# Residual of the second attention layer's first twelve row blocks by an accumulating DMA, with another tile order in the second convolution

## The chip, the cores and the metric

The kernel runs on one core of one Trainium2 chip. The metric is the device time of one execution in microseconds; the time of the kernel before is the median of three runs.

## The reference

The kernel computes four layers on one sequence `x` of 2048 rows by 512 columns in bf16: attention, convolution, attention, convolution. Each layer adds its output to `x`.

```
x = x + _A_ref(_layernorm(x), wqkv, wo)
x = x + _B_ref(_layernorm(x), A, B, C, log_dt, Dskip)
x = x + _A_ref(_layernorm(x), wqkv, wo)
x = x + _B_ref(_layernorm(x), A, B, C, log_dt, Dskip)
```

`_A_ref` is attention with 32 heads of 16 columns over a window of 8 keys that lie 2 rows apart, softmax over those 8, and a projection `wo`. `_B_ref` is a state-space convolution over all 2048 rows: a kernel is made from `A`, `B`, `C` and `log_dt` for every column, and the sequence is convolved with it by a Fourier transform of length 4096. `u * Dskip` is added to its output.

## The kernel before, in words

**Layout.** The residual `x` stays in SBUF as `x_sb`, 128 partitions by 16 row blocks of 512 columns. A "row" below is one of these 16 blocks: 128 partitions x 512 elements, 128 KB in bf16. Row `a` holds the sequence positions 16p + a.

**Order of the work.** Four engines (DVE, ACT, PE, SP) are scheduled by hand: each engine executes its instructions in the order in which the program emits them, and waits on semaphores where an operand is not ready. An instruction that waits holds up everything behind it on its engine.

**Second attention (`LayerA.core`, layer `l == 1`).** After projections and logits comes a loop over n = 0 to 15 (L503 to L538), one row per turn, in the row order `rows = [0, 2, 1, 3, 4, ..., 15]`. A turn emits, in this order:

- DVE: `pv_mult(n)`, the products `pav` of the probabilities with the values (L404). In turns 1, 3, 5 and 7 it is followed by one more product for the last block of logits (L295). Softmax pieces of the last two blocks lie in turns 0 to 11.
- `u_begin` in turns 7, 11 and 15 (L514): mean and variance of four finished rows (0 to 3, 4 to 7, 8 to 11) from the sums `s1` and the sums of squares `s2` that ACT has made; three small DVE instructions (L133, L135, and L140 in turn 7). In turn 7 the power -1/2 is taken on GpSimd (L141), in turns 11 and 15 on ACT as Ln and Exp (L118, L119). `u_end` (L148) follows on DVE, and `u_apply` (L158 on ACT, L160 on DVE) writes the normalised rows.
- PE: `pv_sum(n)`, 32 matmuls with the identity that sum `pav` into `po` (L412); ACT copies it to `oT` (L415).
- `out_proj` of the row of the turn before (L418): PE adds the residual by one matmul of the identity with the 512 columns of `x_sb` (L422), then the four matmuls with `wo` (L424) into the PSUM tile `pq`. For rows 0 to 11, ACT copies `pq` over the row of `x_sb` and sums it (L430), then reads the row back for the sum of squares (L108). For rows 12 to 15 ACT only copies (L428), and DVE makes the statistics (L101).

After the loop a short sequence makes the statistics of rows 12 to 15 and their normalised rows; the convolution waits for the last of them.

**Tiles.** `pav`, `po`, `pq` and `oT` have two buffers each.

**Second convolution (`FftB.run`).** It follows a list of tokens, `ORDER1`, of four kinds of tiles. `U` (16 of them; L756 on PE) is the first transform, copied to SBUF by DVE (`UD`) or ACT (`UA`), L745. `u` (16; L763) is the second transform, which ACT always copies to `ub` (L818); `ub` has three buffers. `m` (16) are two DVE products of `ub` with a part of the filter spectrum (L805); a tile of `ub` is free when its `m` is done. `y` (16; L831 and L832) is the inverse transform, copied by DVE or ACT (L745). `z` (8; L856 and L857) is the last step, which adds into `x_sb` and is followed by a store of the output. Tiles U, u, y and z share four PSUM tiles in turn, so that a tile can begin when the fourth tile before it has been copied. There are two groups of eight: the first eight `y` need `m` 0 to 7, the last eight need all sixteen. In the last `z` tile, marked `B`, DVE and ACT each copy one half.

Of the kernel before, what the change touches and what calls it, by code (L numbers as in the profile page):

```python
# [20 lines left out]
P = 128  # L21
S = 2048
D = 512
# [3 lines left out]
NA = 16  # L27
NDT = 4
# [10 lines left out]
DQG = 64  # L39
# [20 lines left out]
T3 E31D x1 E30A P20 P22  # L60
"""
ORDER1 = """
UD UA UD UA UD UA UD UA UD UA UD u UD m u m UA UA u UD u u m u m u
m m UA u m u m m u u m u yA u m m u yD m yA u yA m u m yA
yA m yD yD yD yA yD yA yA yA yD yA z03D z00D z12D z02D z11D z10D z01A z13B
"""

def build_a_consts(tc, nc, cpool, tpool):
# [38 lines left out]
def row_sumsq(nc, lnst, x_row, a):  # L107
    nc.scalar.activation(lnst["junk"][:], x_row, ACT.Square, accum_out=lnst["s2"][:, a:a + 1])  # L108
# [14 lines left out]
def ln_begin(nc, pool, lnst, a0, a1, eng, rs="pool"):  # L123
    n = a1 - a0
    if eng == "dve":
        ag = pool.tile([P, n, 2], F32, name="ln_ag")
        for a in range(n):
            nc.vector.bn_aggr(ag[:, a, :], lnst["bn"][:, a0 + a, 0, :])
        var, mean, ms = ag[:, :, 1], ag[:, :, 0], -1.0
    else:  # L130
        mean, ms = lnst["s1"][:, a0:a1], -1.0 / D
        msq = pool.tile([P, n], F32, name="ln_msq")
        nc.vector.scalar_tensor_tensor(msq[:], mean, -1.0 / (D * D), mean, ALU.mult, ALU.mult)  # L133
        veps = pool.tile([P, n], F32, name="ln_veps")
        nc.vector.scalar_tensor_tensor(veps[:], lnst["s2"][:, a0:a1], 1.0 / D, msq[:], ALU.mult, ALU.add)  # L135
        var = veps[:]
    if rs == "act":
        return rstd_act(nc, pool, var), mean, ms
    rstd = pool.tile([P, n], F32, name="ln_rstd")
    nc.vector.tensor_scalar(rstd[:], var, EPS, None, ALU.add)  # L140
    nc.gpsimd.tensor_tensor(rstd[:], rstd[:], lnst["mh"][:, 0:n], ALU.pow)  # L141
    return rstd, mean, ms
# [20 lines left out]
class LayerA:  # L163
# [143 lines left out]
    def core(self, x_sb, u, lnp, ev=None, nprod=0):  # L307

        tc, nc, lnst, l = self.tc, self.nc, self.lnst, self.layer
        ident, nident = self.c["ident"], self.c["nident"]  # L310
# [11 lines left out]
        with ExitStack() as c2:  # L322
# [7 lines left out]
            wk = c2.enter_context(tc.tile_pool(name=f"a{l}_wk", bufs=2, reuse_waits="tile"))  # L330
# [87 lines left out]
            def out_proj(a):  # L418
                oT = oTs.pop(a)
                pw = pq_tile()  # L420
                xr = x_sb[:, a, :]
                nc.tensor.matmul(pw[:], lhsT=ident[:], rhs=xr, start=True, stop=False)  # L422
                for ftp in range(NDT):
                    nc.tensor.matmul(pw[:], lhsT=oT[:, ftp, :], rhs=self.wo[:, ftp, :], start=False, stop=(ftp == NDT - 1))  # L424
                if a >= 12:
                    if a >= 14 and l == 1:
                        row_stats(nc, lnst, pw[:], a, "dve")
                    nc.scalar.copy(xr, pw[:])  # L428
                else:
                    nc.scalar.activation(xr, pw[:], ACT.Identity, accum_out=lnst["s1"][:, a:a + 1])  # L430
                    row_sumsq(nc, lnst, xr, a)
# [4 lines left out]
            def u_begin(a0, a1, eng, rs="pool"):  # L436
                lns[a0] = ln_begin(nc, lnp, lnst, a0, a1, eng, rs)
# [64 lines left out]
            rows = [0, 2, 1, *range(3, NA)]  # L502
            for n in range(16):  # L503
                pv_mult(rows[n])
                if n in (0, 8):
                    mx(2 + n // 8)
                if n in (2, 10):
                    recip(2 + n // 8)
                if n in (4, 11):
                    norm_p(2 + n // 8)  # L510
                if n in (1, 3, 5, 7):
                    mult(3, n // 2)
                if n in (7, 11, 15):
                    u_begin(n - 7, n - 3, "act", "act" if n > 7 else "pool")  # L514
                if n in (8, 12):
                    u_end(n - 8)
                if n in (9, 10, 13, 14):
                    b0 = 0 if n < 11 else 4
                    r0 = b0 + (0 if n in (9, 13) else 2)
                    u_apply(b0, range(r0, r0 + 2))  # L520
                if n == 15:
                    x_stats(12)
                event(("p", n))
                if n in (1, 3, 5):
                    q_proj(3, n // 2 + 1)
                pv_sum(rows[n])
                if n in (0, 8):
                    sub_exp(2 + n // 8)
                if n == 15:
                    x_stats(13)  # L530
                    if l == 1:
                        u_end(8)
                        u_apply(8, range(8, 12), "dve")
                if n > 0:
                    out_proj(rows[n - 1])
                if n in (1, 3, 5, 7):
                    lsum(3, n // 2)
                event(("o", n))  # L538
# [7 lines left out]
            pw = pq_tile()  # L546
# [159 lines left out]
class FftB:  # L706
# [129 lines left out]
    def i2(self, g, t, eng):  # L836

        nc, x_sb = self.nc, self.x_sb
        z = self.S[g]["z"]
        dsl = slice(g * DQG * 4, (g + 1) * DQG * 4)  # L840
        if eng == "both":
            for h, e in enumerate(("dve", "act")):
                self.i2_rows(z, t * 4 + 2 * h, 2, dsl, e)
        else:
            self.i2_rows(z, t * 4, 4, dsl, eng)

    def i2_rows(self, z, a0, n, dsl, eng):

        nc, x_sb = self.nc, self.x_sb
        p4 = self.ptile([P, n, DQG * 4])  # L850
        n_add = n if eng == "dve" else 0
        for j in range(n):
            a = a0 + j
            if j >= n_add:
                nc.tensor.matmul(p4[:, j, :], lhsT=self.ident[:], rhs=x_sb[:, a, dsl], start=True, stop=False)
            nc.tensor.matmul(p4[:, j, :], lhsT=self.g2[:, 0, a, :], rhs=z[:, a, :], start=(j < n_add), stop=False)  # L856
            nc.tensor.matmul(p4[:, j, :], lhsT=self.g2[:, 1, a, :], rhs=z[:, NA + a, :], start=False, stop=True)  # L857
        if n_add:
            xr = x_sb[:, a0:a0 + n, dsl]
            nc.vector.tensor_tensor(xr, p4[:], xr, ALU.add)  # L860
        else:
            nc.scalar.copy(x_sb[:, a0:a0 + n, dsl], p4[:])

    def run(self, order, u, done=lambda g, t: None, k=None, late=(), more={}):
        late, cnt = list(late), self.cnt
# [419 lines left out]
def kernel(  # L1285
# [16 lines left out]
    nc = tc.nc  # L1302
# [18 lines left out]
    u = xnT[:].rearrange("p t (b r) -> p (t b) r", r=64).rearrange("p q (a r) -> p q a r", r=4)  # L1321
# [4 lines left out]
    xpool = ctx.enter_context(tc.tile_pool(name="xres", bufs=1))  # L1326
# [59 lines left out]
    with tc.manual_schedule(engines=MAN):  # L1386
        la.front_open()
        ln, agg, pts = {}, {}, {}

        def front_pools():  # L1390
            fb.swap_psum()
            la.front_psum()

        def aggr(b):
            agg[b] = lnp.tile([P, 4, 2], F32, name="ln_ag")
# [22 lines left out]
        fb.run(ORDERF, None, more=front)  # L1418
        la.front_close()
# [60 lines left out]
```

## Time and profile before

| | |
|---|---|
| median of three runs | 429.74 us (429.44 to 429.82) |
| the profiled execution | 429.82 us |
| its span, first to last instruction | 428.0 us |
| so outside the span | 1.82 us |
| mean granted TensorE clock | 0.987 |
| turns of the loop in the second attention | 316.6 to 372 us of the span |
| second convolution, first matmul to end | 376.57 to 428.0 us |

How to read the profile: each engine has its own row. PE is the matrix engine (PEld its loads of weights), DVE the vector engine, ACT the scalar engine, POOL GpSimd, and SP the engine that issues the transfers (SPq its queue). Busy time is the time in which an engine executes an instruction. A row in the timeline gives the start, the duration, the engine, the line of the program, the operation, and the tiles that it writes and reads; a bracket at its end gives the idle time of the engine ahead of it and what ended it. The chain of waits is followed back from the last instruction, at each step to what released it.

### The profile page before, as it was taken

The page shows a single profiled execution, that of the slowest core. Times are in us where ns is not written, and L with a number is a line of the kernel's source. Part 1 is how long each engine was busy: PE and PEld are TensorE (multiplying, and loading weights), DVE is VectorE, ACT ScalarE, POOL GpSimd, SP SyncE. Part 2 cuts the span into 40 slices and gives each one's busy share as a digit, 9 for nine tenths or more (in the row PEclk, how much of TensorE's full clock was granted, in tenths as well). Part 3 has the DMA queues.
Part 4 walks back from the last instruction along what each step waited for, and adds up shares of the span by engine and source line. Part 5 has one row for each costly group of instructions (what it writes and reads, how often), then busy time and mean ns, then how long its engine had stood idle before and what let it go on. Part 6 is the DMA issues. An engine that isn't in the chain of part 4 may idle for free.

```text
span 428.0 us, 12737 instructions
## 1 busy us (share of the span) xinstructions
PE 353.1 (82%) x5506; PEld 264.9 (62%) x5506; DVE 398.1 (93%) x540; ACT 320.9 (75%) x551; POOL 43.9 (10%) x46
## 2 busy tenths in 40 slices
PE   3000159999999899999998999999999999996994
PEld 2000127667755577767887888555666777776993
DVE  8999999999999999996999959899999999899974
ACT  6999998986454389887999978855556568689941
POOL 3000300000598000001300000000000020000000
PEclk9999998999999999999999999999999999998998
DMA  8930732132116743662245592820041056416306
GB/s 213 385 114 12 81 78 69 33 62 64 24 42 186 237 113 107 215 257 102 77 175 188 190 335 43 255 82 2 20 110 46 2 217 240 131 58 175 124 4 196
DMA packets 62466, 54.16 MB, mean 127 GB/s; under 512 B 33893, under 2 KB 50890, under 8 KB 61130
## 3 DMA queue, kind: packets, MB, share of 16 engines
q1 hardware_dynamic: 62266, 53.22, 40.9%
q8 instruction: 43, 0.70, 0.7%
q10 hardware_dynamic: 144, 0.13, 0.2%
q14 instruction: 13, 0.11, 0.1%
HBM read 30.28 MB, written 13.24 MB: 102 GB/s over the span
## 4 chain that ended last, share of the span: by engine, by line
PE 42%; DVE 25%; ACT 10%; issue 4%; DMA 3%; SPq 2%; DVEq 0%; ACTq 0%
PE po L412 7%; DVE pav L404 7%; PE pk L1174 4%; DVE prod L295 4%; DVE a1s L745 4%; PE pq L351 4%; PE pq L424 4%; PE pp L1112 3%; PE pp L242 3%; PE L L302 3%; PE pq L185 3%; DVE t L805 3%; ACT ub L818 2%; PE pb L832 2%; PE pb L831 2%
## 5 line engine op out<-in xcount | busy, mean ns | idle before, releaser
L404 DVE TENSOR_TENSOR pav<-attn,v_ext 128x4096 bf16<-128x4096 bf16 x32 | 72.9, 2282 | 0.0
L295 DVE TENSOR_TENSOR prod<-qT,kT_ext 128x4096 bf16<-128x4096 bf16 x29 | 66.4, 2307 | 0.2
L412 PEld LDWEIGHTS <-pav 128*128 128x128 bf16 x1024 | 58.4, 98 | 12.2 <-DVE pav L404 8.6
L412 PE MATMUL po<-ident,pav 128*128 128x128 bf16 x1024 | 62.5, 219 | 3.8 <-DVE pav L404 3.3
L1102 PE MATMUL pt<-ident,x_blk 128*128 128x128 bf16 x64 | 6.9, 258 | 43.4 <-ACT x_blk L158 43.4
L1014 DVE TENSOR_TENSOR A_t<-A_t,pow_t 128x1024 bf16<-128x1024 bf16 (+4 forms) x46 | 38.4, 873 | 0.2
L1102 PEld LDWEIGHTS <-x_blk 128*128 128x128 bf16 x64 | 5.3, 116 | 46.1 <-ACT x_blk L158 44.4
L818 ACT CAST ub<-pb 128x1024 bf16<-128x1024 f32 x32 | 32.9, 1079 | 1.1 <-PE pb L763 0.5
L763 PE MATMUL pb<-a1s,w_sb 128*128 128x64 bf16 x768 | 29.1, 197 | 5.1 <-ACT a1s L745 2.7
L353 ACT CAST v_ext<-pq 128x512 bf16<-128x512 f32 x32 | 18.8, 586 | 19.3 <-PE pq L351 18.0
L424 PE MATMUL pq<-wop,oT 128*128 128x512 bf16 x128 | 32.8, 379 | 0.0
L302 PEld LDWEIGHTS <-prod 128*128 128x128 bf16 x928 | 27.1, 96 | 8.8 <-DVE prod L295 3.2
L832 PE MATMUL pb<-WpJ,t 128*128 128x128 bf16 x256 | 29.8, 219 | 1.9 <-DVE t L805 1.9
L415 ACT CAST oT<-po 128x512 bf16<-128x512 f32 x32 | 18.6, 580 | 17.0 <-PE po L412 16.9
L745 DVE CAST a1s<-pb 128x1024 bf16<-128x1024 f32 x23 | 27.0, 1214 | 4.3 <-PE pb L756 4.3
L763 PEld LDWEIGHTS <-w_sb 128*128 128x128 bf16 x768 | 26.3, 101 | 7.5 <-issue 5.8
L1112 PE MATMUL pp<-xnT,kT_ext 128*128 128x512 bf16 x96 | 26.6, 405 | 5.2 <-ACT qT L1117 3.2
L831 PE MATMUL pb<-Wp,t 128*128 128x128 bf16 x256 | 30.1, 219 | 0.8 <-ACT ub L818 0.4
L351 PE MATMUL pq<-wv,xnT 128*128 128x512 bf16 x128 | 30.7, 379 | 0.0
L302 PE MATMUL L<-ind,prod 128*128 128x8 bf16 x928 | 27.4, 166 | 1.3 <-DVE prod L295 1.2
L832 PEld LDWEIGHTS <-t 128*128 128x128 bf16 x256 | 24.9, 98 | 3.2 <-DVE t L805 2.1
L745 ACT CAST a1s<-pb 128x1024 bf16<-128x1024 f32 x25 | 24.7, 1033 | 2.3 <-PE pb L756 2.0
(227 smaller groups left out, 863.1 us busy)
## 6 DMA issues: line engine op xcount, KB each, us to landing
w_sb<-w_dram SPq DMA_DIRECT2D x8, 1024.0 KB, 7.6
w_dram<-w_zero SPq DMA_DIRECT2D x1, 4096.0 KB, 14.6
kf_ring<-kf_dram SPq DMA_DIRECT2D x13, 256.0 KB, 3.8
kf_ring<-kf_dram SPq DMA_DIRECT2D x26, 128.0 KB, 3.6
v_ext<-v_ext SPq DMA_DIRECT2D x4, 784.0 KB, 6.2
x_blk<-in_A_x_dram SPq DMA_DIRECT2D x4, 512.0 KB, 4.3
kT_ext<-in_A_wqkv_dram SPq DMA_DIRECT2D x4, 512.0 KB, 10.0
x_sb<-in_A_x_dram SPq DMA_DIRECT2D x4, 512.0 KB, 5.3
```

What stands on the lines that cost most here:

```text
L295: nc.vector.tensor_tensor(pr, self.qT[q][:, ft].unsqueeze(1).to_broadcast([P, W, 4, P]), kap, ALU.mult)
L302: self.nc.tensor.matmul(L[:, al, w, ft * 8:(ft + 1) * 8], lhsT=pr[:, w, al, :], rhs=self.c["ind8"][:], start=(ft == 0 and w == 0 and al % ...
L351: nc.tensor.matmul(pp[:], lhsT=xnT[:, dt, a * P:(a + 1) * P], rhs=wv[:, dt, :], start=(dt == 0), stop=(dt == NDT - 1))
L404: nc.vector.tensor_tensor(pv[:], attn[:, n % 4].unsqueeze(2).to_broadcast([P, W, DH, H]), vap, ALU.mult)
L412: nc.tensor.matmul(po[:, ft, :], lhsT=pvf[:, w, ft * P:(ft + 1) * P], rhs=ident[:], start=(w == 0 and ft == 0), stop=(w == W - 1), skip_gr ...
L424: nc.tensor.matmul(pw[:], lhsT=oT[:, ftp, :], rhs=self.wo[:, ftp, :], start=False, stop=(ftp == NDT - 1))
L745: (self.nc.scalar.copy if eng == "act" else self.nc.vector.tensor_copy)(dst, src)
L763: nc.tensor.matmul(p2[:, j, :], lhsT=self.w2[:, ec * EC + j, :], rhs=a1s[:, ec * EC + j, :], start=True, stop=True)
L818: nc.scalar.copy(ub[:], p2)
L831: nc.tensor.matmul(p3[:, j, :], lhsT=t1[:, dql, :], rhs=wp_r, start=True, stop=False)
L832: nc.tensor.matmul(p3[:, j, :], lhsT=t2[:, dql, :], rhs=wpj_r, start=False, stop=True)
L1112: nc.tensor.matmul(pps[kind, b, ft][:], lhsT=la.wqk[:, dt, c:c + P], rhs=la.xnT[:, dt, b * 512:(b + 1) * 512], start=(dt == 0), stop=(dt = ...
```

## The change

For rows 0 to 11 of the second attention layer the identity matmul (L422) is left out. ACT copies `pq`, now without the residual, to a new tile `ow` with two buffers, and sums it on the way; GpSimd issues a DMA that adds `ow` to the row of `x_sb`. The sum of squares of a row is no longer made directly behind the copy, but two turns later, from the row of `x_sb` that the DMA has written. Since `s1` now holds only the sum of the added part, the mean of the row as it was is kept from the front of the layer (`mean0`) and added by one more DVE instruction in each `u_begin`. In turn 7 the power is taken on ACT instead of GpSimd. In the convolution the token list is another one, and the tile marked `B` is one PSUM tile of four rows instead of two of two rows.

```
 ORDER1:
-UD UA UD UA UD UA UD UA UD UA UD u UD m u m UA UA u UD u u m u m u
-m m UA u m u m m u u m u yA u m m u yD m yA u yA m u m yA
-yA m yD yD yD yA yD yA yA yA yD yA z03D z00D z12D z02D z11D z10D z01A z13B
+UD UA UA UD UA UA UD UA UD UA UD u UD u m UA u u m UA m u u UA m UD m
+u u m m m u u m u m m u u m u m m u yA yA yA m u yA yA yA yA
+m yD yA yD yD yA z00D yD yA z01D yA yA z02D z03D z10D z11D z12A z13B
 ln_begin:
         mean, ms = lnst["s1"][:, a0:a1], -1.0 / D
+        if "mean0" in lnst:
+            nc.vector.scalar_tensor_tensor(mean, lnst["mean0"][:, a0:a1, 0], float(D), mean, ALU.mult, ALU.add)
 out_proj:
-                nc.tensor.matmul(pw[:], lhsT=ident[:], rhs=xr, start=True, stop=False)
+                by_dma = l == 1 and a < 12
+                if not by_dma:
+                    nc.tensor.matmul(pw[:], lhsT=ident[:], rhs=xr, start=True, stop=False)
...
+                if by_dma:
+                    ow = wk.tile([P, D], BF16, name="ow")
+                    nc.scalar.activation(ow[:], pw[:], ACT.Identity, accum_out=lnst["s1"][:, a:a + 1])
+                    nc.gpsimd.dma_start(xr, ow[:], accum_op=ALU.add)
+                elif a >= 12:
 the loop over n:
-                    u_begin(n - 7, n - 3, "act", "act" if n > 7 else "pool")
+                    u_begin(n - 7, n - 3, "act", "act" if n > 7 or l else "pool")
...
                 if n > 0:
                     out_proj(rows[n - 1])
+                if l == 1 and 3 <= n < 15:
+                    row_sumsq(nc, lnst, x_sb[:, rows[n - 3], :], rows[n - 3])
 i2:
+        p4 = self.ptile([P, 4, DQG * 4])
+        n_add = {"dve": 4, "both": 2, "act": 0}[eng]
...
+        if n_add:
+            xr = x_sb[:, t * 4:t * 4 + n_add, dsl]
+            nc.vector.tensor_tensor(xr, p4[:, 0:n_add], xr, ALU.add)
+        if n_add < 4:
+            nc.scalar.copy(x_sb[:, t * 4 + n_add:t * 4 + 4, dsl], p4[:, n_add:4])
```

More of the change, by code (lines that the diff above doesn't have):

```diff
@@ L421, in out_proj @@
                 xr = x_sb[:, a, :]
-                nc.tensor.matmul(pw[:], lhsT=ident[:], rhs=xr, start=True, stop=False)
+                by_dma = l == 1 and a < 12
+                if not by_dma:
+                    nc.tensor.matmul(pw[:], lhsT=ident[:], rhs=xr, start=True, stop=False)
                 for ftp in range(NDT):
-                    nc.tensor.matmul(pw[:], lhsT=oT[:, ftp, :], rhs=self.wo[:, ftp, :], start=False, stop=(ftp == NDT - 1))
-                if a >= 12:
+                    nc.tensor.matmul(pw[:], lhsT=oT[:, ftp, :], rhs=self.wo[:, ftp, :],
+                                     start=(by_dma and ftp == 0), stop=(ftp == NDT - 1))
+                if by_dma:
[3 more added lines that the diff above has]
+                elif a >= 12:
                     if a >= 14 and l == 1:
@@ L840, in i2 @@
         dsl = slice(g * DQG * 4, (g + 1) * DQG * 4)
[L841 to L853, printed above, removed]
+        p4 = self.ptile([P, 4, DQG * 4])
+        n_add = {"dve": 4, "both": 2, "act": 0}[eng]
+        for j in range(4):
+            a = t * 4 + j
             if j >= n_add:
@@ L858, in i2_rows @@
         if n_add:
[L859 to L862, printed above, removed]
+            xr = x_sb[:, t * 4:t * 4 + n_add, dsl]
+            nc.vector.tensor_tensor(xr, p4[:, 0:n_add], xr, ALU.add)
+        if n_add < 4:
+            nc.scalar.copy(x_sb[:, t * 4 + n_add:t * 4 + 4, dsl], p4[:, n_add:4])
     def run(self, order, u, done=lambda g, t: None, k=None, late=(), more={}):
@@ L1388 @@
         ln, agg, pts = {}, {}, {}
+        mean0 = xpool.tile([P, NA, 2], F32, name="ln_mean0")
         def front_pools():
@@ L1394, in aggr @@
         def aggr(b):
-            agg[b] = lnp.tile([P, 4, 2], F32, name="ln_ag")
+            agg[b] = mean0[:, 4 * b:4 * b + 4, :]
             for a in range(4):
@@ L1418 @@
         fb.run(ORDERF, None, more=front)
+        lnst["mean0"] = mean0
         la.front_close()
```

## Prediction

> **What bounds the kernel now.** I read the table of stretches first, then the chain of waits around the changed loop, then the timelines of single engines. In the stretches the columns are: stretch, its length, busy time of PE, PEld, DVE, ACT and POOL, TensorE clock, DMA share and GB/s.
>
> ```profile
> 348.00:355.00 7.00, 6.88 (x96) 5.13 (x93) 6.94 (x7) 5.21 (x12) 1.46 (x1) 1.00 0.99 415
> 355.00:361.00 6.00, 5.87 (x75) 4.38 (x73) 5.92 (x8) 5.30 (x15) 0.00 (x0) 1.00 0.45 184
> 361.00:367.00 6.00, 5.96 (x76) 4.57 (x75) 6.00 (x7) 4.58 (x11) 0.00 (x0) 1.00 0.79 243
> 367.00:376.50 9.50, 9.17 (x90) 5.92 (x88) 7.64 (x21) 5.86 (x14) 0.00 (x0) 1.00 0.36 124
> ```
>
> In the loop DVE is without a gap until its last product ends at 368.55, and PE is nearly as full. So work taken from PE pays only where PE, and not DVE, comes last. The chain (start, length, what) says where:
>
> ```profile
> 355.97 2.19 DVE pav L404
> ...
> 358.21 1.96 PE po L412 x32
> 360.17 0.22 PE pq L422
> 360.39 0.88 PE pq L424 x4
> ...
> 361.28 1.96 PE po L412 x32
> ...
> 372.96 0.71 DVE ln_bn L101
> ```
>
> `po` of turn 11 (358.21) starts when DVE's product is ready, and so does that of turn 12 (361.28: the product of 358.94 ends at 361.22). Whatever PE saves earlier is lost in these waits. From 361.28 on PE sets the pace to 372.96, where DVE's statistics of row 14 begin exactly as PE finishes; the convolution starts at 376.57, 3.6 us behind them.
>
> **The identity matmuls.** One of 512 columns takes 0.22 us of the chain. Twelve go: 12 x 0.22 = 2.6 us of PE. Eleven lie ahead of 361.28, under DVE, and give nothing. Only row 11's, in turn 12, lies behind it: -0.22 us. The waits of PE on DVE grow by the rest.
>
> **The late sums of squares.** The sum of squares of row 7 was done in turn 8; now ACT makes it in turn 10, behind the copy of row 9, and `u_begin` of turn 11 needs it. These are DVE's and ACT's rows there:
>
> ```profile
> 358.07 0.68 DVE L394 TENSOR_TENSOR attn<-ex,rs 128x1024 bf16<-128x1024 bf16 x1
> 358.67 0.15 DVE L133 SCALAR_TENSOR_TENSOR ln_msq<-ln_s 128x4 f32<-128x4 f32 x1
> 358.86 0.16 DVE L135 SCALAR_TENSOR_TENSOR ln_veps<-ln_s,ln_msq 128x4 f32<-128x4 f32 x1
> 358.94 2.28 DVE L404 TENSOR_TENSOR pav<-attn,v_ext 128x4096 bf16<-128x4096 bf16 x1
> ```
> ```profile
> 358.31 0.60 ACT L430 ACTIVATE x_sb<-pq 128x512 bf16<-128x512 f32 x1
> 358.80 0.20 ACT L430 ACTIVATION_READ_ACCUMULATOR x_sb<-pq 128x1 f32 x1
> 359.03 0.63 ACT L108 ACTIVATE ln_junk<-x_sb 128x512 bf16<-128x512 bf16 x1
> 359.57 0.19 ACT L108 ACTIVATION_READ_ACCUMULATOR ln_junk<-x_sb 128x1 f32 x1
> ```
>
> ACT has no idle time from 350.64 but 0.48 us at 355.25, where it waits for PE; an identity matmul less ends this 0.2 us sooner. So its slot for a sum of squares in turn 10 ends at 359.76 - 0.2 = 359.55. DVE, which is in order, waits there with L135 and starts the product of turn 12 at 359.75 instead of 358.94: +0.8 us (this holds the added L133-like instruction of 0.15 us, which runs in the wait). That product is on the chain, so turn 13 starts 0.8 - 0.22 = 0.57 us late, and PE carries this to turn 15.
>
> In turn 15 the same happens with row 11. Its sum of squares now stands behind ACT's copy of row 13, which was at 370.09 and comes at 370.66. It starts at 371.15 and ends some 0.7 us later (0.63 and 0.19, overlapping), at 371.86; DVE's L135 then ends at 372.05, where it was over at 368.8. Behind it wait two statistics (0.6 us each of DVE's time: 373.25), L148 (0.1) and four rows of L160 (1.39): 374.8. Only then can the statistics of row 14 begin, at 372.96 before: +1.85 us, the 0.57 included. What follows is the same chain of 3.6 us. In turn 7, L135 waits until about 345.95, where it ran at 346.03: nothing, with 0.1 us either way.
>
> **The power in turn 7.** ACT gets 0.4 us (Ln and Exp, 0.2 each) ahead of `oT` of turn 7. Behind that copy ACT has 1.49 us idle ahead of 350.64: hidden. Without this cover it would cost 0.4.
>
> **The DMA.** Twelve transfers of 128 KB, SBUF to SBUF, from a queue that the trace of before does not show. They must land in time for ACT: the copy of row a+2 overwrites the tile `ow` of row a, and the sum of squares of row a follows that copy. From the end of one copy to the start of the copy two turns later are 5.0 to 7 us (352.75 to 358.1 for row 7). The nearest rows:
>
> ```profile
> kn<-kn SPq DMA_DIRECT2D x8, 128.0 KB, 2.1
> ...
> kx<-kf_dram SPq DMA_DIRECT2D x4, 128.0 KB, 3.9
> ```
> ```profile
> 170.90 1.02 POOL L141 TENSOR_TENSOR ln_rstd<-ln_rstd,ln_mh 128x4 f32<-128x4 f32 x1 [33.16 <-DVE ln_rstd L140]
> ...
> 346.57 2.89 POOL L141 TENSOR_TENSOR ln_rstd<-ln_rstd,ln_mh 128x4 f32<-128x4 f32 x1 [98.19 <-DVE ln_rstd L140]
> ```
>
> From below: 2.1 us (the same size inside SBUF, idle queues), no cost. From above: twice the busy row, 7.8 us, since the destination is read as well, and 1.9 us because GpSimd's own instruction took 2.89 instead of 1.02 us where a `pav` product ran beside it: 9.7 us. Then a copy comes only every (9.7 + 0.8) / 2 = 5.25 us, against 3.45 us in turns 2 to 12 ((363.08 - 328.57) / 10): 10 x 1.8 = +18 us. I take about 4.5 us, near the busy row plus half a microsecond for GpSimd, and so no cost. Of the two loads beside it, the one of 346 to 356 (0.99 of all DMA engines) makes this least sure. Past POOL's queue nothing is moved; the L141 that stood there is gone.
>
> [...]
>
> **The convolution.** DVE gets one U tile and two y tiles less (1.14 us each), ACT that much more (0.96 each). The end of the last `m` decides when the second eight `y` can start. Before:
>
> ```profile
> 401.90 4.89 DVE L805 TENSOR_TENSOR t<-ub,kf_ring 128x1024 bf16<-128x1024 bf16 x8
> ```
> ```profile
> 403.68 1.09 ACT L818 CAST ub<-pb 128x1024 bf16<-128x1024 f32 x1
> 404.58 2.02 ACT L745 CAST xnT<-pb 128x1024 bf16<-128x1024 f32 x2
> ```
>
> ACT's last `ub` is done at 404.8, DVE's last `m` at 406.8, PE goes on at 406.85. I followed the new list with the durations above, four PSUM tiles and three `ub`. The first `m` starts as before (385.1), DVE then runs 16 `m` of 1.22 and one U, and the `ub` of `m` n waits for `m` n-3: `u` 14 is copied by 402.0. But now three `yA` stand on ACT between it and `u` 15 (402.0 to 404.9), which is done at 405.8: the last `m` ends at 407.0, although DVE has less to do. Four more `yA` follow on ACT until 409.6, and the ninth `y` needs the PSUM tile of the second of them, so PE starts it at 407.8: +0.95 us. From there PE has 8 `y` and 8 `z` of 0.86 us in either list, and the end moves by the same. The two ends: -2.3 us if DVE's lighter load (1.14 x 2 ahead of the last `m`) reached the end, +2 us if all seven `yA` of group 0 delay it. The joined `B` tile changes nothing that I can price above 0.2 us.
>
> **The sum.** Against the profiled execution of 429.82 us (0.08 above the median): 1.85 + 0.95 = 2.8, so 432.6 us.
>
> **Rivals.**
> 1. The transfers land late, and `ow`'s two buffers make ACT wait in turns 3 to 12. It decides from 5.0 us of landing, turn by turn, and in all turns from 6.1 us ((6.1 + 0.8) / 2 = 3.45). At 7 us, between 5.8 (3.9 + 1.9) and 7.8 (twice 3.9), it gives 10 x ((7 + 0.8) / 2 - 3.45) = +4.5 on top, 437.1; at 8 us +9.5, 442. For it: DVE without a gap, full DMA engines. Against: 2.1 to 3.9 us for all such sizes in the trace.
> 2. GpSimd holds DVE up. Beside POOL's L696 the product L295 took up to 2695 ns instead of 2283, and L381 828 instead of 417: 0.41 us for each of 12 issues would be +4.9, 437.5. [...]
> 3. Not slower: the convolution gives its 2.3 us, because ACT's three `yA` are through ahead of `u` 15. It decides if `u` 14 is copied by 400.5 instead of 402.0. With the attention's 1.85 the end is 429.4; if the wait of turn 15 is hidden too, 428.1.
> 4. The change doesn't do what it says: PE is not shorter in the turns, because it waits for DVE as much longer. That holds for eleven of the twelve rows in my forecast already; for the twelfth it is 0.22 us, 432.8, inside the forecast's own range and its chance.
>
> **How the numbers follow.** Forecast (430.7 to 434.5): 0.52. Rival 1: 0.24. Rival 2: 0.08. Rival 3: 0.16, half of it faster. A difference of 0.2%, 0.86 us, is about what a measurement of this kernel can tell from no change, so faster means below 428.9 and slower above 430.6: 0.08, 0.08, 0.84. The range takes rival 3's 429.4 and half of rival 1: 429.2 to 439.5. The forecast's own range is 430.7 to 434.5.
>
> **What would show it.** Right: DVE idle of about 0.8 us ahead of L135 in turn 11 and of 2 to 3 us in turn 15, ended by ACT's sum of squares; PE waits for `pav` that grow to 0.2 us more a turn; landing times under 5 us; `u` 15 copied behind three `y`. Wrong: ACT idle ahead of the copy to `ow`, ended by a DMA; `pav` above 2.3 us; an end of the convolution stage within 51 us of its start.

## The result, and the profile after

The changed kernel takes 435.65 us (median of four, 435.4 to 437.45), beside 429.78 us (429.44 to 430.36) for the kernel before on the same chip: a ratio of 1.0144, interval 1.0115 to 1.0174. (Here and below the ratio is the recorded one, with its 95% interval; it is not exactly the quotient of the two medians.) It is slower by 5.9 us; the forecast was 2.8 us slower, 432.6 us. The sign was right and the size too small by half. The profiled execution took 435.77 us, its span 434.0 us, so 1.8 us lie outside as before.

I cut the two spans at the same events: the start of the product `pav` of turn 0 of the loop, `po` of turns 12 and 15, the first matmul of the convolution, and the last instruction. (Lines of the changed kernel have other numbers: `pav` is L406, `po` L414, the copy to `ow` L432, its DMA L433; inside `u_begin` the instruction that waits for the sums of squares was L135 and is now L137.)

| us | before | after | difference |
|---|---|---|---|
| start of the span to turn 0 | 316.60 | 314.94 | -1.66 |
| turn 0 to `po` of turn 12 | 44.68 | 48.91 | +4.23 |
| `po` of turn 12 to `po` of turn 15 | 8.61 | 11.22 | +2.61 |
| `po` of turn 15 to the convolution | 6.68 | 7.80 | +1.12 |
| convolution, first matmul to end | 51.43 | 51.13 | -0.30 |
| span | 428.0 | 434.0 | +6.0 |

So the loop alone lost 8.0 us. The first thing to look at is the landing of the twelve accumulating transfers. This is the group's line in the list of DMA issues of the changed kernel (last number: median us from issue to landing):

```profile
x_sb<-ow POOLq DMA_DIRECT2D x12, 128.0 KB, 4.5
```

The median is the 4.5 us that I forecast, and it misleads. One by one, in the order of the rows 0, 2, 1, 3, 4, ... 11, they took 4.4, 2.7, 2.7, 2.7, 2.6, 5.1, 7.6, 8.6, 5.1, 4.6, 5.2 and 3.3 us. The two slow ones, rows 6 and 7, were issued at 346.58 and 351.39 us, beside a load of 4 MB that is issued at 344.4 us for the convolution. The chain of waits (start, length, what) goes straight through row 7's:

```profile
351.39 8.63 DMA x_sb<-ow
...
360.10 0.69 ACT ow L432 x2
360.79 0.62 ACT ln_junk L108 x2
361.41 0.02 issue
361.43 0.16 DVE ln_veps L137
361.60 2.21 DVE pav L406
363.80 0.05 issue
363.85 3.60 PE po L414 x32
```

Row 7's transfer lands at 360.02. Only then may ACT write row 9 into the same one of the two `ow` buffers; behind that copy, in order, stands row 7's own sum of squares; for it waits DVE's L137 in turn 11; and behind L137 stands the product of turn 12, for which PE waits. The waits show both ends of it, with the total, the number and the longest in us:

```profile
DVE ln_veps L137 <- ACT ln_junk L108: 6.8, 2, 4.2
...
ACT ow L432 <- DMA x_sb<-ow: 4.1, 2, 2.8
```

The table of stretches of the changed kernel (stretch, length, busy PE, PEld, DVE, ACT, POOL, granted TensorE clock, DMA share, GB/s) shows what comes with the stall and after it:

```profile
345.00:356.00 11.00, 9.98 (x145) 7.57 (x143) 10.93 (x11) 7.58 (x21) 2.26 (x3) 1.00 1.03 355
356.00:364.00 8.00, 2.97 (x38) 2.25 (x39) 3.80 (x8) 4.63 (x14) 1.52 (x3) 0.93 0.68 177
364.00:370.00 6.00, 6.00 (x48) 4.90 (x47) 4.92 (x4) 1.40 (x4) 0.52 (x1) 0.52 0.70 207
```

Before, DVE was busy for 5.92 of the 6 us from 355 to 361 and PE for 5.87. Now DVE is busy for 3.80 of 8 us. The third row is a second loss: PE is busy all the time, but its clock is granted at 0.52 only, behind the pause that it made. PE's own rows give the pause in the bracket and the matmuls at half speed, 3.60 us where `po` takes 1.96:

```profile
356.45 1.96 PE L414 MATMUL po<-ident,pav 128*128 128x128 bf16 x32 [0.56 <-DVE pav L406]
358.25 1.03 PE L428 MATMUL pq<-wop,oT 128*128 128x512 bf16 x4
363.85 3.60 PE L414 MATMUL po<-ident,pav 128*128 128x128 bf16 x32 [4.58 <-DVE pav L406]
367.24 1.91 PE L428 MATMUL pq<-wop,oT 128*128 128x512 bf16 x4
```

Turn 15 is as forecast. L137 waits for row 11's late sum of squares, and the four L162 and the statistics queue behind it (DVE, changed kernel):

```profile
376.51 0.16 DVE L137 SCALAR_TENSOR_TENSOR ln_veps<-ln_s,ln_msq 128x4 f32<-128x4 f32 x1 [2.62 <-ACT ln_junk L108]
376.59 1.28 DVE L101 BATCH_NORM_STATS2 ln_bn<-x_sb 128x6 f32<-128x512 bf16 x2
377.79 0.14 DVE L150 SCALAR_TENSOR_TENSOR ln_nb<-ln_s,ln_rstd 128x4 f32<-128x4 f32 x1
377.97 1.38 DVE L162 TENSOR_SCALAR xnT<-x_sb,ln_rstd,ln_nb 128x512 bf16<-128x512 bf16 x4
```

In the convolution three `yA` copies do stand on ACT ahead of the last `ub`, and DVE waits for it with the last `m` (first ACT, then DVE):

```profile
407.92 2.85 ACT L756 CAST xnT<-pb 128x1024 bf16<-128x1024 f32 x3
410.63 1.06 ACT L829 CAST ub<-pb 128x1024 bf16<-128x1024 f32 x1
```
```profile
411.72 1.29 DVE L816 TENSOR_TENSOR t<-ub,kf_ring 128x1024 bf16<-128x1024 bf16 x2 [1.21 <-ACT ub L829]
```

The last copy of the stage ends 47.04 us after its start, against 45.93: +1.1. Of this 0.5 us are PE's: its tenth `y` starts 31.62 us after the stage's start, against 31.12, and its last matmul 45.43 against 44.91. The other 0.6 us are the joined `B` tile, in which ACT's half now waits for DVE's half, where before the two ended side by side at 422.4 and 422.5 us:

```profile
429.33 0.58 ACT L864 CAST x_sb<-pb 128x512 bf16<-128x512 f32 x1 [0.81 <-DVE x_sb L862]
```

Yet the stage is not longer. The nine stores of the output begin earlier against the last copy, and what follows the last copy is 4.09 us in place of 5.50. I had followed the list to the last copy and not to the last store.

### The profile page after: what moved, and what is told of

Its sections match the earlier page's. It is cut to its first block, busy times and chain, and to the rows that moved or that the text cites. A ratio compares the mean times of both kernels' runs of the same rounds, so it can differ in the third digit from the quotient of the medians.

```text
span 434.0 us, 12771 instructions
## 1 busy us (share of the span) xinstructions
PE 351.8 (81%) x5494; PEld 264.0 (61%) x5494; DVE 394.7 (91%) x539; ACT 322.0 (74%) x556; POOL 51.6 (12%) x57
## 4 chain that ended last, share of the span: by engine, by line
PE 40%; DVE 22%; issue 7%; ACT 6%; DMA 6%; SPq 2%; POOL 1%; DVEq 0%; ACTq 0%; POOLq 0%
PE pk L1176 5%; PE po L414 5%; DVE t L816 5%; DVE pav L406 5%; PE pq L353 4%; PE pp L1114 4%; DVE a1s L756 4%; DVE prod L297 3%; PE pp L244 3%; PE L L304 3%; PE pq L187 2%; PE pq L428 2%; PE pb L842 2%; PE pb L843 2%; DMA x_sb<-ow 2%
## 5 line engine op out<-in xcount | busy, mean ns | idle before, releaser
L406 DVE TENSOR_TENSOR pav<-attn,v_ext 128x4096 bf16<-128x4096 bf16 x32 | 72.9, 2282 | 2.3 <-PE po L414 2.3
L414 PE MATMUL po<-ident,pav 128*128 128x128 bf16 x1024 | 64.6, 223 | 10.2 <-DVE pav L406 10.0
L414 PEld LDWEIGHTS <-pav 128*128 128x128 bf16 x1024 | 60.4, 100 | 19.0 <-DVE pav L406 15.5
L428 PE MATMUL pq<-wop,oT 128*128 128x512 bf16 x128 | 33.7, 387 | 0.0
L774 PE MATMUL pb<-a1s,w_sb 128*128 128x64 bf16 x768 | 27.7, 193 | 4.8 <-ACT ub L829 3.5
L756 DVE CAST a1s<-pb 128x1024 bf16<-128x1024 f32 x22 | 26.1, 1216 | 5.1 <-PE pb L767 5.0
L774 PEld LDWEIGHTS <-w_sb 128*128 128x128 bf16 x768 | 24.8, 98 | 7.5 <-issue 5.9
L756 ACT CAST a1s<-pb 128x1024 bf16<-128x1024 f32 x26 | 25.6, 1043 | 2.3 <-PE pb L767 2.2
```

What stands on the lines that cost most here:

```text
L406: nc.vector.tensor_tensor(pv[:], attn[:, n % 4].unsqueeze(2).to_broadcast([P, W, DH, H]), vap, ALU.mult)
L414: nc.tensor.matmul(po[:, ft, :], lhsT=pvf[:, w, ft * P:(ft + 1) * P], rhs=ident[:], start=(w == 0 and ft == 0), stop=(w == W - 1), skip_gr ...
L756: (self.nc.scalar.copy if eng == "act" else self.nc.vector.tensor_copy)(dst, src)
L774: nc.tensor.matmul(p2[:, j, :], lhsT=self.w2[:, ec * EC + j, :], rhs=a1s[:, ec * EC + j, :], start=True, stop=True)
```

## Theories

**Theory A.** Of the loss, 4.2 us are two transfers that land late because the 4 MB load has the DMA engines; 2.6 us are TensorE's clock behind the pause; 1.1 us are row 11's late sum of squares. **Rivals:** it is the two buffers and not the data; it is GpSimd's queue and not the load; it is the accumulation; the clock falls because of the transfers and not of the pause.

In the results below, "loop" is the time from the product of turn 0 to the convolution's first matmul in the profiled execution (59.97 before, 67.93 after), with its three parts in brackets (44.68, 8.61, 6.68 before): up to `po` of turn 12, from there to `po` of turn 15, and the rest.

## Experiments: each part of the change by itself

**The token list alone,** in the kernel before:

```
-ORDER1, i2 of the kernel before
+ORDER1, i2 of the changed kernel
```

> The kernel before with only the new token list and the joined last tile. Theory A (from the trace after: the last z copy comes 1.2 us later behind the convolution's start, but the stores are spread and the end follows it 1.5 us sooner): -0.3 us, 429.5. Theory B (the forecast's price): +0.95, 430.7.

Measured: 428.83 us beside 429.04, ratio 1.0006 (0.9978 to 1.0034). The last copy comes 47.04 us after the stage's start, as in the changed kernel, and the stage takes 51.41 us (51.43 before). The list is worth nothing either way; that +0.95 did not come is read from the stage, since the interval alone would leave room for it.

**The late sums of squares alone,** in the kernel before, with no DMA:

```
-                    row_sumsq(nc, lnst, xr, a)
+                    if l == 0:
+                        row_sumsq(nc, lnst, xr, a)
...
+                if l == 1 and 3 <= n < 15:
+                    row_sumsq(nc, lnst, x_sb[:, rows[n - 3], :], rows[n - 3])
```

> The kernel before, where only the sum of squares of a row stands two turns later on ACT; no DMA, identity matmuls kept. The forecast's step: +0.8 to 1.0 us in turn 11 (DVE waits at L135) and about +1.05 in turn 15, in all +1.85 to 2.1, 431.6 to 431.9. If the moved statistics are hidden by themselves: 429.8.

Measured: 430.32 us, ratio 1.0022 (1.0003 to 1.0041); loop 61.66, +1.69 (45.25, 8.61, 7.80), so +0.57 in turn 11 and +1.12 in turn 15. DVE's two waits in this kernel:

```profile
359.05 0.16 DVE L135 SCALAR_TENSOR_TENSOR ln_veps<-ln_s,ln_msq 128x4 f32<-128x4 f32 x1 [0.67 <-ACT ln_junk L108]
...
371.51 0.16 DVE L135 SCALAR_TENSOR_TENSOR ln_veps<-ln_s,ln_msq 128x4 f32<-128x4 f32 x1 [2.70 <-ACT ln_junk L108]
```

The forecast had +1.85 with one wait of 0.8 and one of 2 to 3 us.

**No identity matmul,** in the kernel before (the residual of rows 0 to 11 is left out of the output):

```
-                nc.tensor.matmul(pw[:], lhsT=ident[:], rhs=xr, start=True, stop=False)
+                bare = l == 1 and a < 12
+                if not bare:
+                    nc.tensor.matmul(pw[:], lhsT=ident[:], rhs=xr, start=True, stop=False)
...
```

> The kernel before without the twelve identity matmuls; the residual of rows 0 to 11 is left out. The forecast's step: -0.22 us, 429.6, since DVE's products set the pace up to turn 12. If PE sets the pace in all turns: 12 x 0.22 = -2.6 us, 427.2.

Measured: 428.18 us, ratio 0.9967 (0.9949 to 0.9985); loop 59.55, -0.42 of the 2.6 us that the twelve matmuls take. In the loop this is all that leaving them out brings in this schedule, were the DMA free.

## Experiments: the load, or something else?

**DMA for rows 0 to 5 only,** which land ahead of the load or beside its first part; rows 6 to 11 as before the change (and the kept mean is added for rows 0 to 5 alone):

```
...
-                by_dma = l == 1 and a < 12
+                by_dma = l == 1 and a < 6
...
-                if l == 1 and 3 <= n < 15:
+                if l == 1 and 3 <= n and rows[n - 3] < 6:
```

> The changed kernel with the DMA for rows 0 to 5 only; rows 6 to 11 keep the identity matmul and their sum of squares directly behind the copy. Theory A: rows 0 to 5 land in 2.7 to 5 us ahead of their need, DVE waits at no statistic, and the loop is as long as before (59.6 to 60.2 us from turn 0 to the convolution), the time within 0.3% of the kernel before: half of the matmuls gone and nothing gained. Rival (the DMA itself costs, by GpSimd's 0.86 us of issue or by its traffic): at least 2 us above the kernel before.

Measured: 428.87 us beside 428.93, ratio 1.0000 (0.9984 to 1.0015); loop 60.04. The six land in 4.9, 2.7, 2.7, 2.7, 2.6 and 5.8 us, under a DVE without a gap. Half of the change costs nothing and gives nothing.

**The load later,** in turn 13, held back by a store of `s1` of row 11:

```
-        ev = {("p", 8): [lambda: la.load_w2(w2_dram)]}
+        gate = dram.tile([P, 1], F32, name="gate_dram")
+        ev = {("p", 13): [lambda: nc.sync.dma_start(gate[:], lnst["s1"][:, 11:12]), lambda: la.load_w2(w2_dram)]}
```

> The changed kernel with the load of the second-transform weights (4 MB, 0.99 of all DMA engines for 10 us) held back behind the copy of row 11 by a small store ahead of it in its queue. Theory A (the transfers land late because they share the DMA engines with that load): the transfers of rows 5 to 8, which took 5.1 to 8.6 us, land in 2.7 us as those of rows 1 to 4; no copy waits for a DMA; DVE's wait in turn 11 falls from 4.16 to about 0.8 us; PE keeps its clock (it took 3.60 us for a po of 1.96 behind a pause of 4.6 us); 5.5 to 6 us less, 429.7 to 430.5. [...]

Measured: 443.14 us, ratio 1.0301 (1.0268 to 1.0334). The landings are theory A's: rows 0 to 10 take 2.6 to 3.3 us, rows 6 and 7 2.7 us each, and `po` of turn 12 comes 45.27 us after turn 0, with a clock of 1.00. But row 11's transfer, issued at 364.48 between the store and the load, took 14.8 us, and ACT waited for it in turn 14:

```profile
379.61 0.63 ACT L108 ACTIVATE ln_junk<-x_sb 128x512 bf16<-128x512 bf16 x1 [10.03 <-DMA x_sb<-ow]
```

The load moved the stall to the row that it now meets. The experiment has a flaw: my store of 128 pieces of 4 bytes is slow itself (8.4 us to landing in the next run), so that what delays row 11 is load and store together.

**The load last,** in turn 15, behind the same kind of store (now of `s2`):

```
+        ev = {("p", 15): [lambda: nc.sync.dma_start(gate[:], lnst["s2"][:, 11:12]), lambda: la.load_w2(w2_dram)]}
```

> The changed kernel with the load of the second-transform weights held back until the sum of squares of row 11 is written, so that none of the twelve transfers meets it. Theory A (all of the loss beyond the late squares is the meeting with the load; held behind row 11's copy only, it made row 11 land in 14.8 us and cost 10 us in turn 15): all twelve land in 2.6 to 3.5 us, no copy and no sum of squares waits for a DMA, from turn 0 to the convolution 61.1 to 61.7 us (59.97 before, and 1.1 to 1.7 for the late squares), time 1 to 2 us above the kernel before. Rival: the load then comes too late for the first second-transform tile, and the convolution starts to wait: 3 us or more above.

Measured: 437.27 us, ratio 1.0197 (1.0179 to 1.0214). All rows but the first land in 2.6 to 2.9 us and the loop is 61.15, as theory A has it. But the convolution is 58.25 us, 6.8 longer, as the rival has it: the load took 18.6 us (median of its four parts) from issue to landing.

**The same with a store of one element:**

```
-        gate = dram.tile([P, 1], F32, name="gate_dram")
+        gate = dram.tile([1, 1], F32, name="gate_dram")
...
-nc.sync.dma_start(gate[:], lnst["s2"][:, 11:12])
+nc.sync.dma_start(gate[:], lnst["s2"][0:1, 11:12])
```

> The changed kernel with the 4 MB load in turn 15, held back as in the run that loads last, but by a store of one element instead of one of 128 x 1. Theory A (the transfers are late only beside the load): all land in 2.5 to 3.0 us (the first up to 5), the loop is 61.0 to 61.5 us as in the run that loads last (61.15), that is +1.2 for row 11's late sum of squares; the gate lands in about 2 us instead of 8.4, the load in 8 to 10 us instead of 18.6, so that the convolution is 51 to 53 us instead of 58.25, and the time 429.5 to 432 us. Rival (the load itself is too late in turn 15, whatever holds it back): the convolution stays above 55 us and the time above 434 us.

Measured: 430.38 us beside 428.6, ratio 1.0033 (1.0011 to 1.0054); loop 61.43 (45.23, 8.40, 7.80), convolution 51.45. The load lands in 9.8 us (median of its four parts). The list of DMA issues, the longest waits of L137, and the stretch of the stall in this kernel:

```profile
x_sb<-ow POOLq DMA_DIRECT2D x12, 128.0 KB, 2.7
```
```profile
DVE ln_veps L137 <- ACT ln_junk L108: 2.5, 2, 2.3
```
```profile
356.00:364.00 8.00, 6.67 (x91) 5.20 (x91) 7.72 (x9) 5.81 (x18) 2.58 (x3) 1.00 0.24 36
```

DVE is busy for 7.72 us where it was 3.80, and the clock stays at 1.00. With the load out of the way the changed kernel loses 1.8 us, and its loop 1.46 us: the late sums of squares (1.69 by themselves) less what the missing matmuls give (0.42) would be 1.27. So the load is the cause of the late landing, and the landing the cause of the pause and the clock. (The loads of the filter spectrum stand behind the 4 MB load in SP's queue and move with it, from 359.89 to 385.65 us. In the changed kernel row 6 had landed at 354.2 and row 7 at 360.02 us, so for these two it is the 4 MB load.)

**A plain copy in place of the accumulating one,** on the same queue (the residual is left out of rows 0 to 11):

```
-                    nc.gpsimd.dma_start(xr, ow[:], accum_op=ALU.add)
+                    nc.gpsimd.dma_start(xr, ow[:])
```

> The changed kernel with a plain copy in place of the accumulating one on the same queue; the residual of rows 0 to 11 is left out. It measures what accumulation adds. Theory A (landing is set by the shared DMA engines): alone about 2.1 to 2.7 us, beside the load as late as before, 7 to 9 us, so the time stays near 435. Rival (reading the destination is what makes it late): 4 us beside the load, and the time falls to 431 to 432.

Measured, in one execution: 431.97 us, loop 64.11 (47.91, 8.39, 7.81). The landings are 2.0 us where the accumulating ones took 2.7, and 6.7 and 7.7 for rows 6 and 7 (7.6 and 8.6). So the accumulation itself costs 0.7 to 0.9 us, and a plain copy is late too. The time is the one that I had put to the rival, though the landings are theory A's. The 0.9 us were worth more than themselves here: PE's pause was 3.61 us in place of 4.58, and behind it the clock stayed at 1.00.

**The plain copy from SP's queue:**

```
-                    nc.gpsimd.dma_start(xr, ow[:], accum_op=ALU.add)
+                    nc.sync.dma_start(xr, ow[:])
```

> The same plain copy, issued from SP's queue, where the load is issued too; the residual of rows 0 to 11 is left out. Theory A (shared engines): row 6 lands late also from this queue, 5 us or more, and row 7, which stands behind the load in the same queue, not before the load is through, near 355 us of the span. [...]

Measured, in one execution: 436.36 us, loop 68.77. ACT's copy waits even longer:

```profile
361.22 0.60 ACT L432 ACTIVATE ow<-pq 128x512 bf16<-128x512 f32 x1 [4.85 <-DMA x_sb<-ow]
```

Row 6 was issued just ahead of the load and landed in 2.0 us; there my expectation missed. Rows 7 and 8, issued behind it on the same queue, are the late ones. From another queue the transfers beside the load are late as well; but since they also stand behind the load in that queue, this run alone does not acquit GpSimd's. The run with the store of one element does: from GpSimd's queue, under the same products of DVE, all rows but the first land in 2.6 to 2.8 us once the load is gone.

## Experiments: which wait, and can it be mended?

**Four buffers of `ow`:**

```
-                    ow = wk.tile([P, D], BF16, name="ow")
+                    ow = wk.tile([P, D], BF16, name="ow", bufs=4)
```

> The changed kernel with four buffers of ow in place of two. Theory A (the transfers of rows 6 and 7 land late beside the 4 MB load, and two things wait for them: the copy to ow, for the buffer, and the sum of squares of row 7, for the data): the copies no longer wait, but the sum of squares of row 7 still waits for the landing at about 360 us, so that DVE's L137 in turn 11 waits 3.5 to 4.0 us instead of 4.16, and PE's pause is about 4.0 us instead of 4.58. If TensorE's clock stays at 1.00 behind it, the loop is some 64 to 65 us (67.93 in the changed kernel) and the time about 432.5 us; if it falls to about 0.5 as in the changed kernel, 434.5 to 435.5 us. Rival (the two buffers are the cause, the data's own landing is not): the copies set the wait, the loop comes to about 61 us and the time to 429.5 to 430.5 us.

Measured: 433.94 us, ratio 1.011 (1.0076 to 1.0144); loop 65.36 (47.89, 9.67, 7.80). The copies wait no longer; the sum of squares of row 7 now waits for the landing itself:

```profile
357.15 0.59 ACT L432 ACTIVATE ow<-pq 128x512 bf16<-128x512 f32 x1
357.64 0.20 ACT L432 ACTIVATION_READ_ACCUMULATOR ow<-pq 128x1 f32 x1
360.18 0.63 ACT L108 ACTIVATE ln_junk<-x_sb 128x512 bf16<-128x512 bf16 x1 [2.34 <-DMA x_sb<-ow]
```

The rival's 430 us did not come. L137 waited 3.2 us, a little less than I expected. The clock fell, but for half as long as in the changed kernel, so that the time lies between my two cases.

**Every named wait mended:** four buffers; `u_begin`, `u_end` and `u_apply` of rows 4 to 7 one turn later; the sum of squares of row 7 with that of row 8 in turn 11; that of row 11 ahead of the copy of row 13 in turn 14:

```
+                late = 1 if l else 0
-                if n in (7, 11, 15):
+                if n in (7, 11 + late, 15):
...
+                if l == 1 and n == 14:
+                    row_sumsq(nc, lnst, x_sb[:, 11, :], 11)
                 if n > 0:
                     out_proj(rows[n - 1])
-                if l == 1 and 3 <= n < 15:
-                    row_sumsq(nc, lnst, x_sb[:, rows[n - 3], :], rows[n - 3])
+                if l == 1 and 3 <= n < 14:
+                    for r in {10: (), 11: (7, 8)}.get(n, (rows[n - 3],)):
+                        row_sumsq(nc, lnst, x_sb[:, r, :], r)
```

> The changed kernel with four buffers of ow, with mean, variance and normalised rows of rows 4 to 7 one turn later (L137 in turn 12 instead of 11), the sum of squares of row 7 in turn 11 beside that of row 8, and the sum of squares of row 11 ahead of the copy of row 13 in turn 14. Theory A (what the change costs are three waits: the late landing of rows 6 and 7, the half clock that follows from PE's pause, and the late sum of squares of row 11): all three go although the transfers land as late as before, the loop is 60.0 to 61.0 us (59.97 before the change, 67.93 behind it), the time within 0.3% of the kernel before, 428.0 to 430.5 us. Rival (the transfers cost something else as well, such as ACT's or DVE's own time or the load's): the loop stays above 62 us and the time is 2 us or more above the kernel before.

Measured: 429.9 us beside 428.6, ratio 1.0015 (0.9992 to 1.0039), within the 0.3% though the transfers land as late as before (rows 6 and 7 in 7.6 and 8.3 us). The loop is 62.33, not 60 to 61, and by that half of its condition the rival holds: two waits are left.

```profile
DVE ln_veps L137 <- ACT ln_junk L108: 3.2, 2, 2.2
...
ACT ln_junk L108 <- DMA x_sb<-ow: 1.3, 2, 1.0
```

One is 0.98 us in turn 12, where the two sums of squares stand behind a copy on ACT; the other is 2.2 us in turn 15, where row 11's transfer took 5.9 us beside the loads of the filter spectrum, and ACT waited 1.04 us for it. So row 11's transfer meets loads as well. This version does not beat the kernel before either.

## Experiments: the clock

What took the clock: the pause, or the transfers? Three kernels are the kernel before, without any accumulating DMA, and repeat the product of turn 12 (same operands, same result) so that PE has to pause:

```
                 nc.vector.tensor_tensor(pv[:], attn[:, n % 4].unsqueeze(2).to_broadcast([P, W, DH, H]), vap, ALU.mult)
+                for d in ((16, 8) if l == 1 and n == 12 else ()):
+                    a3 = attn[:, n % 4].unsqueeze(2).to_broadcast([P, W, DH, H])
+                    nc.vector.tensor_tensor(pv[:, :, 0:d], a3[:, :, 0:d], vap[:, :, 0:d], ALU.mult)
```

Here `(16,)`, `(16, 8)` and `(16, 16)` stand for one, one and a half, and two products more.

> The kernel before, with the product pav of turn 12 made twice (same operands, same result, 2.28 us more of DVE), so that PE pauses some 2.3 us ahead of po of turn 12. No transfer is added. Theory A (a pause of PE alone takes TensorE's clock, from a length between 2.3 and 4.6 us): too short, the clock stays at 1.00, po takes 1.96 us, the loop is 62.2 us (59.97 + 2.28) and the time some 431.5 to 432 us. Rival (the clock falls because of the transfers): the same; this run is the base of the two that follow.

> The kernel before, with one and a half products more in turn 12 (3.4 us more of DVE), so that PE pauses some 3.4 us. Theory A (the pause alone): the length is at the limit, as in the two runs with 3.58 us (clock down) and 3.61 us (clock up), so either nothing is added to the pause (loop 63.4 us) or about 1.1 us (64.5 us); times that differ by more than 1 us between executions would fit too. Rival (the transfers): loop 63.4 us, clock 1.00.

> The kernel before, with the product of turn 12 made three times (4.56 us more of DVE), so that PE pauses some 4.6 us, as in the changed kernel. Theory A (the pause alone): the clock falls to 0.5 behind the pause, po of turn 12 takes 3.2 to 3.6 us, and the loop is 59.97 + 4.6 + 1.1 to 2.6 = 65.6 to 67.1 us, the time 435 to 436.5 us. Rival (the transfers, or their traffic, take the clock): clock 1.00, po 1.96 us, loop 64.5 us, time about 434 us.

Measured: 432.91, 433.88 and 436.49 us beside 428.55; ratios 1.0094 (1.0061 to 1.0127), 1.0124 (1.0093 to 1.0154) and 1.0166 (1.0135 to 1.0197). The rows of `po` of turn 12, in this order:

```profile
363.93 3.33 PE L415 MATMUL po<-ident,pav 128*128 128x128 bf16 x32 [2.36 <-DVE pav L407]
```
```profile
364.25 3.60 PE L415 MATMUL po<-ident,pav 128*128 128x128 bf16 x32 [3.62 <-DVE pav L407]
```
```profile
367.20 3.46 PE L415 MATMUL po<-ident,pav 128*128 128x128 bf16 x32 [4.69 <-DVE pav L407]
```

All three run behind the pause at half speed, the shortest too, where I had expected full clock. The loops are 64.20, 66.76 and 66.03 us; only the third is as I had expected. The stretch behind the pause of 3.62 us and, to compare, the one behind the 3.61 us of the plain copy from GpSimd's queue:

```profile
364.00:370.00 6.00, 5.75 (x40) 4.37 (x41) 4.92 (x5) 0.58 (x1) 0.00 (x0) 0.50 0.39 125
```
```profile
363.00:367.00 4.00, 4.00 (x62) 3.53 (x63) 4.00 (x3) 1.81 (x6) 0.28 (x1) 1.00 0.91 302
```

So the pause alone takes the clock, and the transfers are not needed for it. But its length does not decide: the same 3.6 us left the clock at 1.00 once and at 0.50 twice. Read in stretches of 1 us, the half clock lasts about 3.4 us (pauses of 2.36, 3.58 and 4.69 us), about 6.8 us (3.62, in the changed kernel 4.58, in the plain copy from SP's queue 5.61 us) or about 13.7 us (9.49 us, in the run that loads in turn 13).

The traces point to what does. In each of them the changes of the clock lie a whole number of 3.41 us apart, so that time can be cut at them into stretches of 3.41 us. (The changed kernel: down at 362.94, up at 369.76, down at 431.21 us, so 2 and 18 times 3.41; the kernel before: 393.27, 396.68 and 423.99 us, 1 and 8 times.) The half clock begins behind a stretch in which PE was busy for 1.05 us or less (the changed kernel, four buffers, the plain copy from SP's queue, the three repeats), here for the pause of 3.62 us:

```profile
360.03:363.44 3.41, 0.60 (x3) 0.10 (x1) 3.34 (x3) 1.56 (x5) 0.00 (x0) 1.00 0.63 181
```

The pause of 3.61 us lies across such a cut (counted from the end of a half clock at 145.9 us), and PE was busy for longer in both stretches:

```profile
357.52:360.94 3.42, 1.79 (x21) 1.05 (x18) 0.45 (x2) 1.51 (x6) 0.54 (x1) 1.00 0.11 23
360.94:364.35 3.41, 1.43 (x26) 1.44 (x27) 3.41 (x3) 1.87 (x6) 0.54 (x1) 1.00 0.85 263
```

The half clock goes on for a second stretch where PE was busy in its first for 2.14 to 2.61 us (plain copy from SP's queue, changed kernel, 3.62 us), and ends where it was busy for 2.71 us or more. So in this loop it is where the pause falls in the stretches, beside its length, that decides between nothing, 3.4 and 6.8 us. This is read from the traces; no run was made to test it. In the convolution, with other matmuls, the half clock also followed stretches with 1.42 and 1.70 us (the run that loads last behind the long store, and the one with the first six rows), and in the front of the kernel before one with 1.34 us (62.21 to 65.62 us of its span), so busy time is not the whole rule.

The kernel before has one such pause too, not in the loop but in its convolution, with a clock of 0.50 behind it:

```profile
393.30 0.43 PE L763 MATMUL pb<-a1s,w_sb 128*128 128x64 bf16 x5 [2.67 <-ACT a1s L745]
```
```profile
393.40:396.60 3.20, 3.20 (x63) 3.20 (x62) 3.20 (x7) 2.97 (x4) 0.00 (x0) 0.50 0.89 249
```

The cost behind the pause (`po` of turn 12 to `po` of turn 15, less 8.61) was 1.64, 2.89 and 1.49 us in the three kernels that repeat the product, 2.61 us in the changed kernel and 1.06 us with four buffers. In the last two the stretch has no identity matmul of row 11 and takes 8.39 us with the clock up (the run that loads last), so that the clock itself cost them 2.83 and 1.28 us. The four executions with the shortest pause fall in two pairs, 434.05 and 433.87, 431.95 and 431.84 us; a clock that falls in some executions and not in others would do that, but only the first of them has a trace.

## Why the forecast was too small

- **The step that failed:** "I take about 4.5 us, near the busy row plus half a microsecond for GpSimd, and so no cost." For rows 6 and 7 it was 7.6 and 8.6 us, beyond the 5 to 7 us that the buffers leave. I had named the load of 346 to 356 as what made the step least sure, and had its DMA share of 0.99 before me, but priced all twelve transfers alike. What I set against rival 1, that all transfers of this size in the trace take 2.1 to 3.9 us, was misread: the list of DMA issues before has two loads of 128 KB above that, with 6.1 us (`wop`) and 5.7 us (`k_rl`). Alone the transfers take 2.7 us, beside the 4 MB load three times as much. Rival 1's mechanism was the true one, in two turns and not in ten: it cost +4.2 us up to `po` of turn 12, with the 0.57 us of the late sums of squares inside. That the median came out at the forecast's 4.5 us is luck: it is the middle of two kinds, five transfers of 2.6 to 3.3 us and seven of 4.4 to 8.6.
- **Missing from the forecast:** the half clock behind PE's pause, +2.6 us. I priced a wait at its length. No pause of this length stands in the loop of the kernel before, and the three repeated products cost 1.5 to 2.9 us more than the pause itself. Yet the profile before had an example in its convolution: a pause of 2.67 us, and the half clock behind it.
- **The late sums of squares:** forecast +1.85, measured +1.69 alone. Right; in the changed kernel turn 15's part is +1.12, turn 11's is hidden under the late landing.
- **The identity matmuls:** forecast -0.22, measured -0.42 of 2.6. Right in kind: PE was not the bound in eleven of twelve turns.
- **The convolution:** forecast +0.95, measured 0. The last copy does end 1.1 us later, but only 0.5 us of it are the list's, and not by the step that I gave: the ninth `y` shows no wait for a PSUM tile, and PE is busy without a gap from the fourth `y` on (8.00 of the 8 us from 409 to 417). The other 0.6 us are the joined `B` tile, which I had priced at nothing. And the stores that follow end no later.
- **Rival 2** (GpSimd holds DVE up) is refuted: `pav` took 2282 ns on the mean before and after, and each issue on GpSimd 0.86 us beside it (the first 1.06). Nor do DVE's products make the transfers late: from 324 to 344 us, with DVE busy for 19.93 of the 20 us and the DMA share at 0.24, those of rows 2, 1, 3 and 4 land in 2.6 to 2.7 us.
- **What stays open:** turn 0 starts 1.66 us earlier in the changed kernel's profile. In nine profiles with `ow` it starts at 314.9 to 316.7 us, in seven without at 315.4 to 318.0, on the mean 1.2 us apart. The diff touches little ahead of it: the `B` tile of a convolution, and where the means are kept. It makes the loss in time (5.9 us) smaller than the loss in the loop (8.0), and I did not try to find its cause.

## What to carry to other kernels

Price a transfer by the stretch in which it is issued, and by what else the DMA engines have there, not by a median over all of its kind; and give its reader the slack of the slowest. Moving the reader (429.9 us) and moving the load (430.38 us) each won back nearly all of the loss; which is cheaper these two runs don't tell. A wait on the engine ahead of PE can cost more than its length: here pauses from 2.36 us on took the clock for 3.4 us or more, one of 3.61 us did not. Work taken from an engine that waits in most turns is worth only the turns in which it doesn't wait: 0.42 of 2.6 us here.

## What the runs showed of the hardware

- An accumulating DMA of 128 KB inside SBUF landed in 2.7 us, a plain one from the same queue in 2.0 us; beside a 4 MB load (355 GB/s in all in that stretch) they took 7.6 to 8.6 and 6.7 to 7.7 us.
- A store of 128 pieces of 4 bytes took 8.4 us to land, and a load of 4 MB issued behind it 18.6 us, against 9.8 us behind a store of one element.
- PE's half clock lasted 3.4, 6.8 or 13.7 us in these runs, that is one, two or four times 3.41 us, and a pause of 2.36 us was enough for it in one. In this loop it began behind stretches of 3.41 us with 1.05 us or less of PE's work, and not behind one with 1.43 us.
